# Weight sums on GpSimd alone, hidden tiles paired, and one sum moved back to VectorE: a tuned attention and mixer kernel

## The chip, the cores and the metric

The kernel runs on one core of a Trainium2 chip. The core's engines are TensorE (PE in the profile; its weight loads, PEld, run beside its products), VectorE (DVE), ScalarE (ACT), GpSimd (POOL) and SyncE (SP), which here issues nearly all DMA transfers. Each engine works through its own instructions in the order in which they are written and waits on semaphores for the others.

The metric is the device time of one execution in microseconds (us). Beside the plain runs there is one profiled execution, whose trace gives every instruction's start and duration. Times in the text that look like "at 296.46" are microseconds from the first instruction of that execution. The TensorE clock granted is given as a share of full speed.

## The reference: banded attention, then a mixer

For 4 batches, 8 heads, 768 positions and heads 64 wide, attention sees a band of 31 neighbours and 24 block summaries (maxima of the keys and means of the values over 32 positions):

```python
k_sum = k.reshape(B, H, nb, block, D).max(axis=3)
v_sum = v.reshape(B, H, nb, block, D).mean(axis=3)
scores_l = scale * np.matmul(q, k.transpose(0, 1, 3, 2))
mask_l = np.abs(pos[:, None] - pos[None, :]) < window
scores_s = scale * np.einsum('bhsd,bhnd->bhsn', q, k_sum) + np.log(block)
a = softmax over both
x = np.matmul(a, v_all)
```

The result x (768 positions by 512 channels in each batch) goes through a mixer over positions and one over channels:

```python
h = np.maximum(xt @ w_tok1, 0.0) @ w_tok2        # 768 -> 256 -> 768
u = x + h.transpose(0, 2, 1)
h2 = np.maximum(u @ w_ch1, 0.0) @ w_ch2          # 512 -> 1536 -> 512
return u + h2
```

## The kernel before

**Numbers in two parts.** For accuracy most float32 operands are held as two tiles, a rounded high part and the rest. Three products (high by high, high by low, low by high) stand for one. To "split" a tile means one ScalarE copy and one VectorE or POOL subtraction.

**Batches and slots.** The kernel works in three steady batches b = 0, 1, 2 and a last one. The channel mixer of a batch takes 24 slots: two halves of the positions (512 and 256 of them), each with the 12 tiles f of the 1536 hidden channels. A slot is `ch1` (products hp, into h, line 852) and `ch2` (products acc, line 895). Beside it run the attention steps of batch b + 1, in which `scores` begins with a small clear of a tile e on POOL (MEMSET, line 409), then the first mixer of batch b + 1 (`tok1x`: POOL makes the low parts of xs and ws at line 733 for the products t1q at line 747; `tok2`: products up, line 791). After half 0, `finish` adds the results on VectorE (line 926) and POOL (ot, line 934), and stores them. During batch 0 all weights are loaded as 64-bit words, converted and split; they stay in SBUF, 12 tiles `w1_t[f]` and 12 tiles `w2_t[f]`, tags "w1" and "w2".

**The last batch.** The channel mixer of batch 3 is done with Strassen's scheme in Winograd's form: the matrices are cut into 2 by 2 blocks, and 7 products of blocks do the work of 8. It needs four sums of weight blocks for each of 6 pairs of hidden tiles and both weights: 12 groups s_w_k, w = 1, 2 and k = 0 to 5. `weight_sums` makes a group in ten steps of 128x256 elements (`between`: a tensor_tensor on POOL, line 973, or a scalar_tensor_tensor on VectorE, line 975) and stores it to DRAM ("sums"). `last_mix` reads them back. Its first phase runs k = 0 to 5 (products pa, pb, pc). Each step k uses its two tiles of the first weights for the last time. Their buffers, tag "w1", are a ring of 12, taken in order by the weights of the second phase: `second_loads` reads 21 tiles, r (copies of the second weights) and rs (sums, which `parted` splits on ScalarE and VectorE). The second phase is seven sets of 36 products: qa, qb (sums s2), qc (s3), qb (s1), qa, qb (s4), qc. The right sides of these come from `second`, which splits them on ScalarE and VectorE (x, xs). The last set's right side, t4, is one more subtraction per k, th <- hb, th, done in place after t2 has been split.

**What sets the order.** Work is not issued where the program names it. `Plan` records each piece with its engine, an assumed duration, a rank and its reads and writes, then runs a list schedule and writes the instructions of each engine in the planned order. `rank` decides among pieces that are ready (R_H first, R_BACK last; the sums have R_BACK). `behind` lets a piece be planned only after another, here the slot's ch1 (`state["gate"]`); on the chip it leaves no wait, only a place in the order. A buffer of a ring (tag, number of buffers) is taken over when all users of its previous tile are done, and on the chip this is a wait at the first instruction that touches it, with everything behind it on that engine.

**The sums before.** `SUMS` names the slots: 14 and 17 in batch 0, then 6, 8, 10, 13, 15 and 6, 8, 10, 12, 14. In half 0 a group's result takes two tiles of the ring "t1" (4 buffers, also used by t1 in `tok1x`), in half 1 one tile of the ring "h". Five of the ten steps are POOL's, five VectorE's.

Of the kernel before, what the change touches and what calls it, by code (L numbers as in the profile page):

```python
# [15 lines left out]
ALU = mybir.AluOpType  # L16
# [23 lines left out]
HL = ((0, 0), (0, 1), (1, 0))  # L40

# [148 lines left out]
def tile_attention_mixer(  # L190
# [759 lines left out]
    HALF = NF // 2  # L950
    sd, wd = {}, {}

    def blocks(w, k):

        a, c = ((w1_t, w2_t)[w - 1][f] for f in (k, k + HALF))
# [23 lines left out]
    def weight_sums(w, k, tag):  # L979
# [4 lines left out]
        if tag == "t1":  # L984
            z = [sbuf([P, 2, 256], tag, f"s_{w}_{k}_{n}", 4) for n in range(2)]
            at = [(z[i // 2], i % 2) for i in range(4)]
        else:
            z = sbuf([P, 4, 256], tag, f"s_{w}_{k}", 2)
            at = [(z, i) for i in range(4)]
# [8 lines left out]
        def step(eng, i, left, right, op):  # L998
            add(
                eng, 0.78 if eng == "pool" else 0.38,  # L1000
                lambda: between(eng, own(i)[0](), left[0](), right[0](), op),
                reads=left[1] + right[1], writes=[at[i]], rank=R_BACK, behind=gate,
            )

        step("pool", 0, part("21", 0), part("22", 0), ALU.add)
        step("pool", 0, own(0), part("21", 1), ALU.add)
        step("pool", 0, own(0), part("22", 1), ALU.add)
        step("dve", 2, part("11", 0), part("21", 0), ALU.subtract)
        step("dve", 2, own(2), part("11", 1), ALU.add)
        step("dve", 2, own(2), part("21", 1), ALU.subtract)  # L1010
        step("pool", 1, own(0), part("11", 0), ALU.subtract)
        step("pool", 1, own(1), part("11", 1), ALU.subtract)
        step("dve", 3, part("12", 0), own(1), ALU.subtract)
        step("dve", 3, own(3), part("12", 1), ALU.add)
        for n in range(2):
            view = (lambda n=n: z[n].t) if tag == "t1" else (lambda n=n: z.t[:, 2 * n : 2 * n + 2])
            add(
                "sp", 0.06,
                lambda n=n, view=view: nc.sync.dma_start(
                    out=away.t[:, 2 * n : 2 * n + 2], in_=view()  # L1020
# [78 lines left out]
    def last_mix():  # L1099
# [71 lines left out]
        def first(k, name, bank_, rhs, start):  # L1171
# [4 lines left out]
            else:  # L1176
                slot, c0 = w1_t[k + HALF * (name[0] == "2")], 2 * (name[1] == "2")
# [8 lines left out]
        def second_loads():  # L1186
            for name, _, _ in SECOND:
                for m in range(HALF // 2):
                    slot = wring[name, m] = sbuf([P, 2, 2, 256], "w1", f"r{name}_{m}", NF, F32R)
                    for j in range(2):  # L1190
# [6 lines left out]
                        else:  # L1197
                            away = wd[k + HALF * (name[1] == "2")]
# [86 lines left out]
        def second(name, rhs, to, k):  # L1285
# [5 lines left out]
            if rhs == "t4":  # L1291
                both("pool", src, (hB[k], 0), src, ALU.subtract, R_LATER)
# [380 lines left out]
```

## Time and profile before

| | us |
|---|---|
| median of 3 runs (577.3 to 581.13) | 580.96 |
| profiled execution | 584.92 |
| its span, first to last instruction | 582.4 |
| TensorE busy | 562.4 (97%) |
| VectorE busy | 389.2 (67%) |
| ScalarE busy | 257.4 (44%) |
| POOL busy | 226.0 (39%) |

The mean granted TensorE clock was 0.985. By the trace's rows, the three steady batches reach from about 120 to 485, the first phase of `last_mix` from 485 to 531, its second phase from 527 to 579.

How to read the rows: a row of groups gives line, engine, operation, output <- inputs by the program's names, shapes and count; then busy us in all, mean ns of one, and the idle time of the engine just before them with what ended it. A row of waits gives who waited for whom: us in all, times, the longest. A row of the chain of waits or of the timeline begins with the start and the duration in us; in square brackets stands the engine's idle time before it. A row of windows gives the stretch, its length, and for each engine the busy time and the number of instructions in it, then the clock, the DMA engines' busy share and GB/s. A busy TensorE is not TensorE at its peak, since ends of matmuls are modelled.

### The profile page before, as it was taken

Reading aid. Unit: us, or ns where it says so; the run is one execution under the profiler, and the core shown is the slowest. Engines: PE = TensorE matmul, PEld = TensorE weight load, DVE = VectorE, ACT = ScalarE, POOL = GpSimd, SP = SyncE. Lnnn points to the kernel's source line nnn. Section 1 sums busy time; section 2 is a strip of 40 time slices with the busy share of each in tenths; the row PEclk is TensorE's granted clock in tenths of the full one; section 3 lists DMA queues with packets and bytes.
Section 4 is the critical chain, followed back from the end, with each engine's and each line's share of the span. In section 5 each row is a group of like instructions: output and inputs, shape, how many; then the busy total and the mean of one; then the engine's idle time right before and its main releaser. Section 6 shows DMA issues by size and latency. Waiting matters only on the chain.

```text
span 582.4 us, 12756 instructions
## 1 busy us (share of the span) xinstructions
PE 562.4 (97%) x4629; PEld 491.2 (84%) x4629; DVE 389.2 (67%) x1036; ACT 257.4 (44%) x789; POOL 226.0 (39%) x271
## 2 busy tenths in 40 slices
PE   7899999989989999999999999999999999999897
PEld 4698888768988987878799997777789999999797
DVE  4688889997575346466657526465544884788985
ACT  4668665537373424232242315332233243557452
POOL 0225577753351610203169410032249512446511
PEclk9879999999989999999999999999999999999999
DMA  8953668653747116767685606777687654435321
GB/s 270 319 169 96 198 199 255 214 186 131 224 147 218 35 43 184 181 199 197 210 256 142 129 12 185 151 185 186 184 225 228 178 227 134 148 117 176 130 98 68
DMA packets 133774, 99.52 MB, mean 171 GB/s; under 512 B 88272, under 2 KB 112464, under 8 KB 133712
## 3 DMA queue, kind: packets, MB, share of 16 engines
q1 hardware_dynamic: 133568, 98.52, 57.2%
q8 instruction: 36, 0.59, 0.4%
q14 instruction: 26, 0.21, 0.1%
q10 hardware_dynamic: 144, 0.20, 0.1%
HBM read 68.60 MB, written 28.31 MB: 166 GB/s over the span
## 4 chain that ended last, share of the span: by engine, by line
PE 69%; DVE 12%; DMA 8%; issue 3%; POOL 3%; ACT 2%; SPq 1%; DVEq 0%; ACTq 0%; POOLq 0%
PE acc L895 19%; PE hp L852 18%; PE av L557 4%; PE t1q L747 4%; PE sc L426 3%; DMA w<-in_w_ch 3%; PE pb L1131 3%; PE up L791 3%; PE qa L1131 2%; DMA away<-e 2%; PE pc L1131 2%; PE pa L1131 2%; PE qb L1131 2%; PE qc L1131 2%; DVE wb L1453 2%
## 5 line engine op out<-in xcount | busy, mean ns | idle before, releaser
L895 PE MATMUL acc<-h,w 128*128 128x512 f32 (+1 forms) x864 | 166.0, 341 | 2.5 <-DVE h L869 2.1
L852 PE MATMUL hp<-u,w 128*128 128x512 f32 (+1 forms) x864 | 163.7, 339 | 0.0
L895 PEld LDWEIGHTS acc<-h,w 128*128 128x128 f32 x864 | 133.2, 189 | 23.8 <-DVE h L869 2.8
L852 PEld LDWEIGHTS hp<-u,w 128*128 128x128 f32 x864 | 133.0, 188 | 20.5 <-issue 1.3
L450 ACT ACTIVATE e<-e,den 128x120 f32<-128x120 f32 x192 | 73.3, 384 | 60.2 <-DVE den L440 58.0
L869 DVE SCALAR_TENSOR_TENSOR h<-hp,h 128x512 fp32r<-128x512 f32 (+1 forms) x72 | 39.8, 553 | 67.6 <-ACT h L864 67.4
L864 ACT ACTIVATE h<-hp 128x512 fp32r<-128x512 f32 (+1 forms) x72 | 35.0, 486 | 104.3 <-PE hp L852 98.2
L440 DVE CUSTOM_DVE_ANT_0 e<-sc,mask_sb 128x120 f32<-128x120 f32 x192 | 41.4, 277 | 11.9 <-PE sc L426 10.8
L934 POOL TENSOR_TENSOR ot<-ot,u 128x512 f32<-128x512 f32 (+1 forms) x24 | 23.8, 1018 | 64.2 <-DVE ot L926 57.1
L1482 POOL TENSOR_TENSOR w<-wb,w 128x256 fp32r<-128x256 f32 x48 | 37.6, 802 | 18.1 <-ACT w L1476 17.8
L409 POOL MEMSET e<- 128x48 f32 x16 | 2.2, 138 | 107.6 <-DMA away<-e 42.6
L791 PE MATMUL up<-wt,t 128*128 128x512 f32 (+2 forms) x192 | 39.2, 345 | 0.4 <-DVE u L808 0.3
L973 POOL TENSOR_TENSOR s<-s,w 128x256 f32<-128x256 f32 x48 | 36.8, 768 | 3.4
L450 ACT ACTIVATION_READ_ACCUMULATOR e<-e,den 128x1 f32 x192 | 36.1, 188 | 0.0
L791 PEld LDWEIGHTS up<-wt,t 128*128 128x128 f32 x192 | 30.3, 189 | 3.8 <-DVE u L808 0.8
L733 POOL TENSOR_TENSOR xs<-x,xs 128x512 fp32r<-128x512 f32 x18 | 24.2, 1343 | 19.3 <-ACT xs L728 19.3
L557 PEld LDWEIGHTS av<-v,eT 120*64 120x64 f32 x768 | 25.1, 143 | 7.7 <-issue 4.7
L557 PE MATMUL av<-v,eT 120*64 120x64 f32 x768 | 27.6, 230 | 3.7 <-issue 2.2
L426 PE MATMUL sc<-k,q 64*64 64x120 f32 x768 | 28.9, 277 | 1.8 <-PE et L488 0.7
L426 PEld LDWEIGHTS sc<-k,q 64*64 64x64 f32 x768 | 21.3, 136 | 10.7 <-issue 6.6
L747 PE MATMUL t1q<-xs,ws 128*128 128x256 f32 x216 | 28.8, 284 | 0.1
L1476 ACT ACTIVATE w<-wb 128x256 fp32r<-128x256 f32 x48 | 18.0, 412 | 24.0 <-DVE wb L1453 23.9
(130 smaller groups left out, 900.0 us busy)
## 6 DMA issues: line engine op xcount, KB each, us to landing
w<-in_w_ch SPq DMA_DIRECT2D x48, 256.0 KB
k<-in_kw SPq DMA_DIRECT2D x16, 720.0 KB
v<-in_vw SPq DMA_DIRECT2D x32, 288.0 KB
q<-in_q SPq DMA_DIRECT2D x16, 384.0 KB
sums<-s SPq DMA_DIRECT2D x24, 256.0 KB
away<-e SPq DMA_DIRECT2D x16, 384.0 KB
eT<-away SPq DMA_DIRECT2D x64, 96.0 KB
w2d<-w SPq DMA_DIRECT2D x12, 512.0 KB
```

The costliest lines, as they stand in the source:

```text
L426: nc.tensor.matmul(tiles[j].t[c * QT : (c + 1) * QT, i * NC : (i + 1) * NC], lhsT=qt.t[rows, t * QT : (t + 1) * QT], rhs=kt.t[rows, t, :], ...
L440: nc.vector.tensor_tensor_reduce(out=e.t[:, j, i * P : i * P + NC], in0=tiles[j].t[:, i * NC : (i + 1) * NC], in1=mask_sb[:, mv, :], op0=A ...
L450: nc.scalar.activation(ei, ei, AF.Exp, bias=den_t[n].t[:, 1, T : T + 1], scale=-1.0, accum_out=den_t[n].t[:, 0, T : T + 1],)
L557: nc.tensor.matmul(pv[cs, T], lhsT=eT[:NC, T % (TT // 2), cs], rhs=v.t[:NC, 2 * T + c], start=True, stop=True,)
L747: nc.tensor.matmul(pt.t[:, 2 * P * k : 2 * P * (k + 1)], lhsT=ws[:, wp, T, ks], rhs=xs[:, xp, T], start=(c == 0 and k == 0 and T == 0 and ...
L791: nc.tensor.matmul(pt.t[:, :nt], lhsT=t1.t[:, part, ks], rhs=wt2[w].t[:, k, h0 : h0 + nt], start=(far and k == 0 and i == 0), stop=(k == D ...
L852: nc.tensor.matmul(pt.t[:, :nt], lhsT=w1_t[f].t[:, w, c], rhs=us[c].t[:, part], start=(i == 0), stop=(i == len(ops) - 1),)
L869: lambda: nc.vector.scalar_tensor_tensor(out=h.t[:, 1], in0=pt.t[:, :nt], scalar=0.0, in1=h.t[:, 0].bitcast(F32), op0=ALU.max, op1=ALU.sub ...
L895: nc.tensor.matmul(slot.t[:, c0 : c0 + nt], lhsT=w2_t[f].t[:, w, o * P : (o + 1) * P], rhs=h.t[:, part], start=(f == 0 and w == 0 and part ...
L973: nc.gpsimd.tensor_tensor(out=out_, in0=left, in1=right, op=op)
L1131: nc.tensor.matmul(bank_.t[:, :HS], lhsT=w(i), rhs=x(j), start=first and n == 0, stop=True, skip_group_check=True,)
L1482: lambda hi=hi, lo=lo, source=source: nc.gpsimd.tensor_tensor(out=lo(), in0=source(), in1=hi().bitcast(F32), op=ALU.subtract),
```

## The change

Three things change.

1. All ten steps of a group are POOL's. The groups stand one per slot in slots 6 to 11 (half 0) of batch 1, for the first weights, and of batch 2, for the second. Batch 0 has none. All results take the ring "t1". The assumed duration of a step is 0.82 instead of 0.78 (POOL) and 0.38 (VectorE).
2. The hidden tiles f are loaded in the order of channel blocks 0, 6, 1, 7, 2, 8 and so on, so that the pair of `last_mix`'s step k is tiles 2k and 2k + 1 instead of k and k + 6.
3. t4 is VectorE's instead of POOL's.

```diff
-        a, c = ((w1_t, w2_t)[w - 1][f] for f in (k, k + HALF))
+        a, c = ((w1_t, w2_t)[w - 1][f] for f in (2 * k, 2 * k + 1))
...
-        if tag == "t1":
-            z = [sbuf([P, 2, 256], tag, f"s_{w}_{k}_{n}", 4) for n in range(2)]
-            at = [(z[i // 2], i % 2) for i in range(4)]
-        else:
-            z = sbuf([P, 4, 256], tag, f"s_{w}_{k}", 2)
-            at = [(z, i) for i in range(4)]
+        z = [sbuf([P, 2, 256], "t1", f"s_{w}_{k}_{n}", 4) for n in range(2)]
+        at = [(z[i // 2], i % 2) for i in range(4)]
...
-        step("dve", 2, part("11", 0), part("21", 0), ALU.subtract)
+        step(2, part("11", 0), part("21", 0), ALU.subtract)
...
-                slot, c0 = w1_t[k + HALF * (name[0] == "2")], 2 * (name[1] == "2")
+                slot, c0 = w1_t[2 * k + (name[0] == "2")], 2 * (name[1] == "2")
...
-                            away = wd[k + HALF * (name[1] == "2")]
+                            away = wd[2 * k + (name[1] == "2")]
...
-                both("pool", src, (hB[k], 0), src, ALU.subtract, R_LATER)
+                both("dve", src, (hB[k], 0), src, ALU.subtract, R_LATER)
...
-        fs, ws = slice(f * P, (f + 1) * P), slice(2 * f * P, 2 * (f + 1) * P)
+        at = f // 2 + HALF * (f % 2)
+        fs, ws = slice(at * P, (at + 1) * P), slice(2 * at * P, 2 * (at + 1) * P)
...
-    SUMS = ((14, 17), (6, 8, 10, 13, 15), (6, 8, 10, 12, 14))
...
-            if slot in SUMS[b]:
-                n = len(sd)
-                weight_sums(1 + n // HALF, n % HALF, "t1" if half == 0 else "h")
+            if b and HALF <= slot < NF:
+                weight_sums(b, slot - HALF)
```

The planner then writes other orders. In the names below the first number after s, e or ot is left out: s_4_0 is the first tile of group k = 4, w a weight tile, e a tile of attention weights, and the last number is a running one.

POOL before, batch 1, from the last sums of half 0 to the first mixer's low parts:

```order
L973 TENSOR_TENSOR s_4_0_3581<-w_10_1601 128x256
L973 TENSOR_TENSOR s_4_0_3581<-s_4_0_3581,w_10_1601 128x256
L409 MEMSET e_0_3590 128x6x8
L973 TENSOR_TENSOR s_4_0_3581<-s_4_0_3581,w_10_1601 128x256
L973 TENSOR_TENSOR s_4_0_3581<-s_4_0_3581,w_4_1210 128x256 x2
L409 MEMSET e_1_3723 128x6x8
L934 TENSOR_TENSOR ot_0_0_3788<-ot_0_0_3788,u_0_0_2731 128x512
```

POOL now, the same place:

```order
L410 MEMSET e_1_3713 128x6x8
L973 TENSOR_TENSOR s_4_1_3709<-s_4_1_3709,w_8_1500 128x256
L973 TENSOR_TENSOR s_4_1_3709<-s_4_1_3709,w_9_1556 128x256
L973 TENSOR_TENSOR s_4_0_3667<-s_4_0_3667,w_8_1500 128x256 x2
L973 TENSOR_TENSOR s_4_1_3709<-w_8_1500,s_4_0_3667 128x256
L973 TENSOR_TENSOR s_4_1_3709<-s_4_1_3709,w_8_1500 128x256
L973 TENSOR_TENSOR s_5_0_3792<-w_11_1661 128x256
L935 TENSOR_TENSOR ot_0_0_3786<-ot_0_0_3786,u_0_0_2707 128x512
```

Between the clear of e_1 and ot no sum stood before; now seven steps do. From batch 1's third clear to ot there are 12, 19, 10 and 7 steps behind one clear each, where there were 1, 7, 3 and 0; three steps stand in front of that clear and nine behind ot, xs and ws. In batch 2 the counts are 2 in front of the first clear after slot 6, then 8, 18, 10, 13 and nine behind ot.

VectorE before, in the second phase of `last_mix`, around the right sides of qb (xs <- th) and of qc (xs <- ha):

```order
L975 SCALAR_TENSOR_TENSOR xs_1_6601<-th_6176,xs_1_6601 128x384
L975 SCALAR_TENSOR_TENSOR rs_0_6511<-rs_0_6511 128x2x256
L975 SCALAR_TENSOR_TENSOR xs_2_6614<-th_6335,xs_2_6614 128x384
L975 SCALAR_TENSOR_TENSOR rs_1_6513<-rs_1_6513 128x2x256
L975 SCALAR_TENSOR_TENSOR xs_3_6643<-th_6335,xs_3_6643 128x384
L975 SCALAR_TENSOR_TENSOR xs_4_6649<-th_6491,xs_4_6649 128x384
L975 SCALAR_TENSOR_TENSOR rs_2_6515<-rs_2_6515 128x2x256
L975 SCALAR_TENSOR_TENSOR xs_5_6663<-th_6491,xs_5_6663 128x384
L975 SCALAR_TENSOR_TENSOR rs_0_6517<-rs_0_6517 128x2x256
L975 SCALAR_TENSOR_TENSOR xs_0_6675<-ha_6075,xs_0_6675 128x384
```

VectorE now, the same place:

```order
L975 SCALAR_TENSOR_TENSOR xs_1_6616<-th_6185,xs_1_6616 128x384
L975 SCALAR_TENSOR_TENSOR th_6185<-hb_6157,th_6185 128x384
L975 SCALAR_TENSOR_TENSOR xs_2_6631<-th_6352,xs_2_6631 128x384
L975 SCALAR_TENSOR_TENSOR th_6352<-hb_6239,th_6352 128x384
L975 SCALAR_TENSOR_TENSOR xs_3_6653<-th_6352,xs_3_6653 128x384
L975 SCALAR_TENSOR_TENSOR th_6352<-hb_6321,th_6352 128x384
L975 SCALAR_TENSOR_TENSOR xs_4_6659<-th_6519,xs_4_6659 128x384
L975 SCALAR_TENSOR_TENSOR th_6519<-hb_6408,th_6519 128x384
L975 SCALAR_TENSOR_TENSOR xs_5_6669<-th_6519,xs_5_6669 128x384
L975 SCALAR_TENSOR_TENSOR th_6519<-hb_6492,th_6519 128x384
L975 SCALAR_TENSOR_TENSOR xs_0_6681<-ha_6081,xs_0_6681 128x384
L975 SCALAR_TENSOR_TENSOR rs_2_6590<-rs_2_6590 128x2x256
```

The splits of rs that stood between the xs have moved ahead, into the first phase, but for one here and one in front of the first xs; in their places stand the six t4 (th <- hb, th).

More of the change, by code (lines that the diff above doesn't have):

```diff
@@ L40 @@
 HL = ((0, 0), (0, 1), (1, 0))
+HALF = NF // 2
 HI_MAX = 122879.9921875
@@ L947, in store @@
         )
-    HALF = NF // 2
     sd, wd = {}, {}
     def blocks(w, k):
-        a, c = ((w1_t, w2_t)[w - 1][f] for f in (k, k + HALF))
+        a, c = ((w1_t, w2_t)[w - 1][f] for f in (2 * k, 2 * k + 1))
         lo, hi = slice(0, 256), slice(256, 512)
@@ L977, in between, with weight_sums @@
             )
-    def weight_sums(w, k, tag):
+    def weight_sums(w, k):
         blk, keys = blocks(w, k)
@@ L996, in own, with step @@
             return (lambda: slot.t[:, j]), [at[i]]
-        def step(eng, i, left, right, op):
+        def step(i, left, right, op):
             add(
-                eng, 0.78 if eng == "pool" else 0.38,
-                lambda: between(eng, own(i)[0](), left[0](), right[0](), op),
+                "pool", 0.82,
+                lambda: between("pool", own(i)[0](), left[0](), right[0](), op),
                 reads=left[1] + right[1], writes=[at[i]], rank=R_BACK, behind=gate,
             )
-        step("pool", 0, part("21", 0), part("22", 0), ALU.add)
-        step("pool", 0, own(0), part("21", 1), ALU.add)
-        step("pool", 0, own(0), part("22", 1), ALU.add)
-        step("dve", 2, part("11", 0), part("21", 0), ALU.subtract)
[L1009 to L1014, printed above, removed]
+        step(0, part("21", 0), part("22", 0), ALU.add)
+        step(0, own(0), part("21", 1), ALU.add)
+        step(0, own(0), part("22", 1), ALU.add)
+        step(2, part("11", 0), part("21", 0), ALU.subtract)
+        step(2, own(2), part("11", 1), ALU.add)
+        step(2, own(2), part("21", 1), ALU.subtract)
+        step(1, own(0), part("11", 0), ALU.subtract)
+        step(1, own(1), part("11", 1), ALU.subtract)
+        step(3, part("12", 0), own(1), ALU.subtract)
+        step(3, own(3), part("12", 1), ALU.add)
         for n in range(2):
-            view = (lambda n=n: z[n].t) if tag == "t1" else (lambda n=n: z.t[:, 2 * n : 2 * n + 2])
             add(
                 "sp", 0.06,
-                lambda n=n, view=view: nc.sync.dma_start(
-                    out=away.t[:, 2 * n : 2 * n + 2], in_=view()
+                lambda n=n: nc.sync.dma_start(
+                    out=away.t[:, 2 * n : 2 * n + 2], in_=z[n].t
                 ),
```

## The prediction

> **What bounds the kernel now.** I read the page first, then busy time by windows, TensorE's own waits, the chain of waits, the groups by line and form, and VectorE's and POOL's timelines.
>
> ```profile
> span 582.4 us, 12756 instructions
> PE 562.4 (97%) x4629; PEld 491.2 (84%) x4629; DVE 389.2 (67%) x1036; ACT 257.4 (44%) x789; POOL 226.0 (39%) x271
> ```
>
> The windows, one row for each stretch:
>
> ```profile
> core 0: us, PE busy (x) PEld busy (x) DVE busy (x) ACT busy (x) POOL busy (x), PEclk, DMA share, GB/s
> ...
> 210.00:295.00 85.00, 85.00 (x678) 67.83 (x678) 50.20 (x180) 26.85 (x108) 14.51 (x25) 1.00 0.65 180
> ...
> 430.00:470.00 40.00, 39.48 (x333) 38.20 (x331) 26.26 (x46) 15.44 (x34) 30.50 (x28) 1.00 0.76 231
> ...
> 485.30:531.00 45.70, 45.70 (x263) 45.70 (x262) 34.43 (x60) 24.25 (x56) 19.29 (x19) 1.00 0.47 148
> 531.00:550.00 19.00, 15.82 (x84) 13.85 (x82) 18.45 (x21) 11.63 (x24) 14.13 (x11) 1.00 0.46 146
> ```
>
> TensorE is the bound: 562.4 of 582.4 us. The change leaves its products in number and shape as they are, so only its idle 20 us are at stake, and most of them lie where the change does nothing (the start, the weight loads). In the batches it hardly idles: not at all in 210:295, 0.5 us in 430:470. The window 531:550 differs: TensorE idles 3.2 us and VectorE is busy 18.45 of 19. There VectorE is the bound. TensorE's waits and the chain of waits say the same:
>
> ```profile
> PE qb L1131 <- DVE xs L975: 2.0, 3, 0.8
> ...
> PE qc L1131 <- DVE xs L975: 1.2, 2, 0.6
> ...
> PE et L488 <- DVE x L570: 1.0, 2, 0.7
> ```
>
> ```profile
> 170.39 1.49 DVE s L975
> ...
> 173.56 0.86 DVE s L975
> ...
> 531.61 4.25 PE qa L1131 x24
> ...
> 553.21 6.24 PE qb L1131 x36
> ```
>
> In last_mix the products qa end at 531.61 + 4.25 = 535.86, and the second set of 36 qb starts at 553.21. Between them stand 72 products, two sets of 36. The set that begins at 553.21 takes 6.24 (the 24 qa, at 4.25, make it 6.4), so 12.5 of those 17.35 us are work and **4.9 are waiting**, for VectorE's split xs. The other wait that bears on this change is in batch 0: transposes of e wait 1.0 us in all for VectorE's x, and on the chain in front of that x stand steps of the weight sums (1.49 and 0.86).
>
> **The change part by part.** First the prices.
>
> ```profile
> L973 POOL TENSOR_TENSOR s<-s,w 128x256 f32<-128x256 f32 x48 | 36.8, 768 | 3.4
> L975 DVE SCALAR_TENSOR_TENSOR s<-s,w 128x256 f32<-128x256 f32 x36 | 21.2, 590 | 0.8
> L975 DVE SCALAR_TENSOR_TENSOR s<-w,s 128x256 f32<-128x256 f32 x12 | 7.1, 595 | 0.8 <-POOL s L973 0.8
> ...
> L973 POOL TENSOR_TENSOR th<-hb,th 128x384 f32<-128x384 f32 x12 | 15.4, 1293 | 2.0 <-DVE xs L975 1.5
> L975 DVE SCALAR_TENSOR_TENSOR xs<-th,xs 128x384 fp32r<-128x384 f32 x12 | 10.4, 884 | 0.3 <-ACT xs L1044 0.3
> L975 DVE SCALAR_TENSOR_TENSOR x<-ha,x 128x384 fp32r<-128x384 f32 x6 | 3.1, 552 | 0.2 <-ACT x L1044 0.2
> L975 DVE SCALAR_TENSOR_TENSOR rs<-rs 128x512 fp32r<-128x512 f32 x12 | 11.0, 919 | 0.6 <-ACT rs L1143 0.5
> 550.33 0.68 DVE L975 SCALAR_TENSOR_TENSOR rs<-rs 128x512 fp32r<-128x512 f32 x1
> 171.80 0.71 DVE L563 SCALAR_TENSOR_TENSOR rec<-den 128x6 f32<-128x6 f32 x1
> 298.94 0.15 DVE L563 SCALAR_TENSOR_TENSOR rec<-den 128x6 f32<-128x6 f32 x1
> ```
>
> *Sums off VectorE.* Twelve groups of ten steps; half of the 120 steps leave VectorE (60 at about 0.59, some 35 us) and come to POOL at 0.768. Nearly all of what VectorE loses lay beside TensorE's work, since TensorE hardly waits there. What it pays: in batch 0 the sums vanish from slots 14 and 17, and with them the 1.0 us of TensorE's wait for x. I take −1.0 (between 0, if another step is then late, and −2.4, the two sums on the chain). Around the end of batch 2, where VectorE also loses sums, TensorE idles 0.5 us; that is the most that goes there, and I leave it to pay for what comes next.
>
> *Sums on POOL.* Each of batches 1 and 2 now has 60 steps there, from slot 6 on. Whether they fit is read from POOL's own row of waits and steps, since POOL works in written order: the clears of e (MEMSET) must wait for their slot, and sums stand between them.
>
> ```profile
> 253.61 0.14 POOL L409 MEMSET e<- 128x48 f32 x1 [12.30 <-DVE s L975]
> ...
> 263.14 0.14 POOL L409 MEMSET e<- 128x48 f32 x1 [8.71 <-PE av L557]
> 264.04 3.25 POOL L973 TENSOR_TENSOR s<-s,w 128x256 f32<-128x256 f32 x4
> 280.27 0.14 POOL L409 MEMSET e<- 128x48 f32 x1 [11.47 <-DMA away<-e]
> 289.22 0.14 POOL L409 MEMSET e<- 128x48 f32 x1 [6.50 <-PE av L557]
> 296.46 2.55 POOL L934 TENSOR_TENSOR ot<-ot,u 128x512 f32<-128x512 f32 x2 [7.10 <-ACT e L450]
> 388.15 0.14 POOL L409 MEMSET e<- 128x48 f32 x1 [3.98 <-DMA away<-e]
> 410.13 0.14 POOL L409 MEMSET e<- 128x48 f32 x1 [11.05 <-DMA away<-e]
> 430.80 2.54 POOL L934 TENSOR_TENSOR ot<-ot,u 128x512 f32<-128x512 f32 x2 [12.74 <-DVE ot L926]
> 456.19 3.72 POOL L973 TENSOR_TENSOR s<-s,w 128x256 f32<-128x256 f32 x4
> ```
>
> A step costs 3.25 / 4 = 0.81 from start to start. In batch 1 the new order puts 12, 19, 10 and 7 steps behind the four clears that now start at 253.61, 263.14, 280.27 and 289.22. From 253.7, 12 steps end at 263.5 (0.4 behind the next clear's time), 19 at 279.0 (clear at 280.27), 10 at 288.5 (289.22), 7 at 295.0, in front of ot at 296.46. The nine left over stand behind the first three pairs xs, ws, where ten stood before. In batch 2 it is 8 and 18 steps from 388.15 to 410.13 (26 × 0.81 = 21.1, of 22.0), then 10 and 13 up to ot at 430.80 (23 × 0.81 = 18.6, of 20.7). So POOL is full and in time, by one or two us in forty: I take 0 for the halves' first parts. If it is late, xs and ws behind ot are late, and TensorE's t1q with them. If steps keep the 3.72 / 4 = 0.93 that the last four took, beside VectorE's sums, ot comes 2.2 late in batch 1 and 3.3 in batch 2: 5.5 us at most. At the end of batch 2 six steps instead of three stand in front of the second half's pairs xs, ws, 3 × 0.81 = 2.4 us; TensorE has had hp and acc moved ahead there, so I take 0.5, the idle time saved above, and let the two cancel (0 to 2.4).
>
> The Trainium skill speaks against this move: in "GPSIMD Engine Reference", Engine selection, it gives elementwise work on a tile to VectorE and calls GpSimd about twice as slow with two inputs. The rows agree in direction (0.768 against 0.59). By that rule POOL, not TensorE, would set the pace of these slots; what that gives here is the second rival.
>
> *VectorE beside a full POOL.* A reciprocal's first step, rec, took 0.71 beside POOL's sums and 0.15 without. With 8 of these in each batch, 8 × 0.56 = 4.5 us come onto VectorE, which has 35 idle in 210:295. I take 0.
>
> *t4 on VectorE.* Six of the twelve th on POOL, 1.29 each, go to VectorE. No row has t4 there; its nearest is x<-ha, same size and operation, 0.552 (upper bound: 0.884, as xs runs now beside POOL). So VectorE gets 6 × 0.55 = 3.3 more in the stretch where it is the bound, but the splits xs next to it fall from 0.884 to 0.552.
>
> *Channel tiles in pairs.* The order of f in ch1 and ch2 costs nothing: same tiles, same loads, others' columns. Its effect is in last_mix: step k frees two neighbouring slots of the ring "w1" instead of slots k and k + 6, so loads r and rs, which take that ring in order, come twice as early, and their splits on VectorE with them. Of six rs splits that stood among the twelve xs behind qa, two remain.
>
> *The sum for 535.86 to 553.21.* For the first set VectorE has 6 xs and 6 t4, 12 × 0.552 = 6.6, against TensorE's 6.24; for the second 6 xs, one rs (0.68) and two sums out_a (0.55 each by x<-ha): 5.1 against 6.24. Before it was 12 × 0.884 + 6 × 0.919 + 1.1 = 17.2, which is the 17.35 seen. So TensorE is the bound again but for 0.4 us at the start, and 4.9 − 0.4 = 4.5 go; with POOL's last th still beside the first xs, I take **−4.3** (0 to −4.9). The five other rs splits fall into 485:531, where VectorE is busy 34.4 of 45.7: 5 × 0.919 = 4.6 more, 85%. A bank's evacuation can then stand behind a split: I take +0.5 (0 to 2).
>
> The sum: −1.0 − 4.3 + 0.5 − 0.5 + 0.5 = **−4.8 us**. The profiled execution took 584.92 us, its span 582.4; it becomes about 580.1. The median of the runs shown is 580.96, 4 us lower, and 580.96 − 4.8 = 576.2, 0.8% less. A measurement of this kernel tells about 1% (5.8 us) from no change.
>
> **The rivals.**
>
> *VectorE stays the bound in last_mix.* For it: 11.7 us of work against 12.5 is close, the first phase gets fuller, and xs could keep 0.884 while POOL ends its last th. Against: six POOL instructions that ran beside xs are gone. With xs and t4 at 0.884 the first set takes 12 × 0.884 = 10.6, 4.4 more than TensorE's 6.24; 0.5 of the 4.9 is gained, and with batch 0 the time is about 579.5. Chance 0.2.
>
> *POOL runs late by contention* (0.93 for a step): TensorE has 0.7 to 1.5 us to spare at t1q, so of 5.5 about 4 reach it: 576.2 + 4 = 580. Chance 0.15.
>
> *Stores hold up the sums: slower.* Tiles of the sums stand in the ring "t1" of four, two for each group, so group k + 2 waits until the stores of group k have landed, and SP issues those in written order, behind loads of k and q.
>
> ```profile
> 381.64 6.46 DMA away<-e
> ...
> 466.61 3.90 DMA w2d<-w
> ```
>
> Sizes, by the page's list of DMA issues:
>
> ```profile
> k<-in_kw SPq DMA_DIRECT2D x16, 720.0 KB
> q<-in_q SPq DMA_DIRECT2D x16, 384.0 KB
> sums<-s SPq DMA_DIRECT2D x24, 256.0 KB
> away<-e SPq DMA_DIRECT2D x16, 384.0 KB
> ```
>
> The store away<-e landed 6.46 us after its issue, w2d<-w after 3.90. From a tile's last step to its next first step there are 12 steps, 9.7 us. While issue and landing stay below that, nothing waits; with 3.5 us more on SP in front of them, every reuse (four in each batch) costs up to 3 us, 12 in a batch. About 1.5 are spare before ot and 0.7 at t1q, so TensorE loses some 10 in each batch: 576.2 + 20 = 596, or 586 if half of the reuses are late. It decides at 9.7 us from a tile's last step to its landing. For it speaks that in each batch some stores stand right behind a k and a q: 720 + 384 + 256 KB at the 180 GB/s of 210:295 are 7.6 us. Against: the others don't, and 6.46 and 3.90 stay below 9.7. Chance 0.15.
>
> **How the numbers follow.** Forecast 0.5, VectorE still the bound 0.2, POOL late 0.15, stores 0.15. The likeliest gives 576.2; its own range goes from 573 (2.4, 4.9 and 0.5 gained, nothing paid) to 580 (most of the bounds paid). The other cases are 579.5, 580 and 586 to 596. With the 4 us by which the runs shown differ, 571 to 585 holds all but the stores' case and a tail. More than 1% faster means below 575.2: somewhat under half of the forecast, 0.22, and 0.06 by the spread of runs from the neighbours, 0.28. Slower by over 1% (above 586.8) is the stores' case but for its mild end, and accidents of order: 0.14. Within 1%: 0.58.
>
> **What would show it.** In the changed profile: TensorE's waits for xs (2.0 and 1.2) gone or below 1 in all, and the next 36 qb starting about 13 us after qa's end instead of 17.35; xs at 0.55 to 0.65; rs splits before qa. No wait of et for x in batch 0. POOL busy without a gap from slot 6 to ot in batches 1 and 2, with ot at most 1 us later than VectorE's part of it, and t1q not waiting for ws. If POOL's sums wait for DMA sums<-s in most groups, the stores' case is right. I am wrong altogether if TensorE waits at t1q or at av in batch 1 or 2, or if VectorE's evacuations hold banks in 485:531.

## The result, and the profile after

The changed kernel takes 571.42 us (median of 4 runs, 569.56 to 572.01). The kernel before took 579.91 in its four runs (577.3 to 581.13). The ratio is 0.9854, 95% interval 0.9809 to 0.9899: 8.5 us less, between 5.9 and 11.1. By the prediction's bound of 1% that is faster. The prediction was 4.8 us less, 576.2. Its wide range, 571 to 585, just holds the time; the likeliest case's own range, 573 to 580, doesn't, and "within 1%", which had the highest chance (0.58), didn't come. Two executions of e6 below, 675.51 us at a TensorE clock of 0.75 and 1308.95 us, are slow ones, and no figure here rests on them.

The profiled execution of the changed kernel took 569.56 us, 1.9 below its median; that of the kernel before took 584.92, 5.0 above its own. The spans therefore differ by 14.8 us, which is more than the change is worth. Some of this lies in the first 60 us, where the instructions are the same: TensorE's clock there was 0.87 and 0.90 before (windows 0:30 and 30:60) and 1.0 after. Some lies in the second half of batch 0, which is taken up under e4.

The page's first lines after:

```profile
span 567.6 us, 12757 instructions
PE 552.1 (97%) x4629; PEld 485.3 (85%) x4629; DVE 355.6 (63%) x982; ACT 258.2 (45%) x789; POOL 258.9 (46%) x325
```

VectorE has lost 33.6 us and POOL has gained 32.9. To see where TensorE gained, I cut each span at the starts of the same products: the first hp of each half, the first pa, and the second set of qb behind qa in `last_mix`. A row of this table is the time from one such start to the next, read from the timelines; the last column is the rest of the span. (The first hp of batch 0 starts at 68.48, so the steady batches begin there and not at about 120.)

```
                    to     batch 0        batch 1        batch 2        pa to   rest
                 1st hp  half 0 half 1  half 0 half 1  half 0 half 1  2nd qb
before            68.48   69.07  74.67   80.97  53.28   81.12  57.57   67.88  29.39
changed           65.53   68.56  71.01   80.97  52.50   81.05  55.24   63.22  29.55
```

Between batch 1 and the end there are four differences: -0.78 in the second half of batch 1, -0.07 and -2.33 in batch 2, and -4.66 in `last_mix`. The first half of batch 1 is the same to the hundredth of a microsecond, although POOL now does all its sums there. The windows of the second half of batch 2, before and then after (the columns are those of the prediction's windows):

```profile
427.60:485.17 57.57, 56.52 (x470) 54.73 (x468) 35.41 (x67) 20.34 (x46) 30.50 (x28) 1.00 0.63 197
```

```profile
419.62:474.86 55.24, 55.24 (x470) 54.50 (x468) 28.57 (x57) 20.60 (x46) 29.71 (x28) 1.00 0.66 207
```

TensorE does the same 470 products, in a somewhat different order (the planner's two orders part in the second half of batch 1). Of the 2.33 us only 57.57 - 56.52 = 1.05 stood as idle time before; the other 1.28 was in its busy time. The time from the start of one product to the start of the next shows where: before, ten such steps are longer than usual (0.12 for hp and acc, 0.17 for up) by 2.3 us together, and each is at a product that waits for u or h, or right beside one. All other steps take the same time in both profiles to within 0.03 us in all, so the order itself costs nothing. Three rows of TensorE's timeline before show the waits, and three of VectorE's show who was late:

```profile
459.85 5.76 PE L791 MATMUL up<-wt,t 128*128 128x384 f32 x30 [0.27 <-DVE u L808]
470.17 0.50 PE L895 MATMUL acc<-h,w 128*128 128x256 f32 x2 [0.40 <-ACT h L864]
471.03 1.46 PE L895 MATMUL acc<-h,w 128*128 128x256 f32 x10 [0.35 <-DVE h L869]
...
453.87 2.66 DVE L975 SCALAR_TENSOR_TENSOR u<-u,u 128x384 fp32r<-128x384 f32 x1 [1.48 <-ACT u L818]
...
457.33 0.97 DVE L975 SCALAR_TENSOR_TENSOR s<-w,s 128x256 f32<-128x256 f32 x1
...
470.56 0.41 DVE L869 SCALAR_TENSOR_TENSOR h<-hp,h 128x256 fp32r<-128x256 f32 x1
```

From 456 to 474 VectorE's timeline shows no idle time. Seven steps of sums stand there, from 456.92 to 463.8, among the evacuations of up (u), t and hp (h), and single instructions beside POOL's took up to 2.66 us. After, the sums are not there, and VectorE waits for ScalarE in front of an h instead:

```profile
457.30 0.42 DVE L870 SCALAR_TENSOR_TENSOR h<-hp,h 128x256 fp32r<-128x256 f32 x1 [0.22 <-ACT h L865]
```

In batch 1 four long steps make 0.7 of the 0.78 us: two at `up`, which waits for VectorE's x behind steps of the sums, and two at `t1q`, which waits for POOL's ws behind four steps of sums. No view of waits lists them, since each gap is under 0.15 us.

In `last_mix`, the chain of waits after:

```profile
521.30 4.24 PE qa L1126 x24
525.54 6.36 PE qb L1126 x36
531.90 6.34 PE qc L1126 x36
538.24 6.29 PE qb L1126 x36
```

From qa's end (525.54) to the second qb (538.24) it is 12.70 us where it was 17.35. TensorE's waits for xs, 2.0 and 1.2 before, are gone from its list. VectorE's timeline at that place:

```profile
523.03 1.31 DVE L975 SCALAR_TENSOR_TENSOR xs<-th,xs 128x384 fp32r<-128x384 f32 x1
524.38 1.26 DVE L975 SCALAR_TENSOR_TENSOR th<-hb,th 128x384 f32<-128x384 f32 x1
525.56 0.55 DVE L975 SCALAR_TENSOR_TENSOR xs<-th,xs 128x384 fp32r<-128x384 f32 x1
526.14 0.56 DVE L975 SCALAR_TENSOR_TENSOR th<-hb,th 128x384 f32<-128x384 f32 x1
```

The first two run beside POOL's last two instructions there, th and ha, and take 1.3; the later ones of these twelve take 0.55.

### The profile page after: what moved, and what is told of

The parts are those of the page before. It is cut to its first block, busy times and chain, and to the rows that moved or that the text cites. A ratio compares the mean times of both kernels' runs of the same rounds, so it can differ in the third digit from the quotient of the medians.

```text
span 567.6 us, 12757 instructions
## 1 busy us (share of the span) xinstructions
PE 552.1 (97%) x4629; PEld 485.3 (85%) x4629; DVE 355.6 (63%) x982; ACT 258.2 (45%) x789; POOL 258.9 (46%) x325
## 4 chain that ended last, share of the span: by engine, by line
PE 76%; DVE 11%; DMA 6%; ACT 3%; issue 2%; POOL 1%; SPq 1%; ACTq 0%; DVEq 0%
PE acc L896 21%; PE hp L853 20%; PE t1q L748 5%; PE up L792 4%; PE av L558 4%; PE pb L1126 3%; PE qb L1126 3%; PE sc L427 3%; DMA w<-in_w_ch 3%; PE qa L1126 2%; PE pc L1126 2%; PE pa L1126 2%; PE qc L1126 2%; DVE wb L1449 2%; ACT e L451 1%
## 5 line engine op out<-in xcount | busy, mean ns | idle before, releaser
L973 POOL TENSOR_TENSOR s<-s,w 128x256 f32<-128x256 f32 x84 | 61.7, 741 | 5.0
```

What stands on the lines that cost most here:

```text
L973: nc.gpsimd.tensor_tensor(out=out_, in0=left, in1=right, op=op)
```

## The experiments

The theory after the result: the gain is in four places (batch 0, the two second halves, `last_mix`), and in the second halves it comes from no sums standing there, not from POOL doing them. The rivals: that POOL alone matters; that batch 0 holds most of it; that POOL or the stores are near a limit. Each ratio is to the kernel before on the same chip. The table of stages, for all of them whose profile is used:

```
                    to     batch 0        batch 1        batch 2        pa to   rest
                 1st hp  half 0 half 1  half 0 half 1  half 0 half 1  2nd qb
e1_t4             65.05   68.66  70.31   80.97  53.96   80.58  57.56   63.93  29.75
e2_pairs          68.25   70.50  72.70   80.97  53.28   80.83  57.56   64.72  29.72
e3_sums           65.64   68.80  72.01   80.97  52.50   80.98  55.24   67.90  29.74
e4_b0             65.24   68.75  71.59   80.97  53.28   80.33  57.58   67.93  29.63
e5_t4pool         67.59   69.11  70.11   80.97  52.50   80.77  55.24   64.75  29.51
e7_allpool        65.97   70.85  70.07   80.97  52.50   81.68  57.15   67.94  29.51
e8_twice          65.34   69.49  71.39   80.97  54.70   81.61  58.80   63.25  29.62
e9_stores         67.02   69.23  71.76   78.36  59.82   81.86  61.31   75.28  29.52
e10_stores2       67.42   68.61  69.92   80.97  52.50   82.12  61.83   63.25  29.64
e11_half0         64.94   69.51  72.41   80.00  53.56   80.75  55.22   63.25  29.63
e12_mixed         65.27   70.56  71.61   80.00  53.90   80.66  56.22   63.21  29.40
```

(In the runs e11 and e12, 24 of TensorE's products sc stand in the second half of batch 1 instead of the first, so the two halves are to be read together.)

### One part at a time

**e1_t4**: the kernel before with t4 on VectorE.

```diff
-                both("pool", src, (hB[k], 0), src, ALU.subtract, R_LATER)
+                both("dve", src, (hB[k], 0), src, ALU.subtract, R_LATER)
```

> The kernel before with one change: t4 on VectorE. From the end of the 24 qa to the start of the second set of qb it took 17.35 us before and 12.70 after. If the splits xs are slow because POOL works beside them, VectorE has 14 xs and t4 at 0.55, six rs at 0.68 to 0.92 and 1.1 for two sums: 12.9 to 14.3, so 3.0 to 4.4 us go and the ratio to before is 0.993 to 0.995. If 0.884 is what an xs costs by itself, t4 only adds to VectorE: 19 us there, 1.7 us slower, ratio 1.003. Nothing else changes.

577.73 us, ratio 0.9949 (0.9922 to 0.9977). From pa to the second qb it is 63.93 instead of 67.88, so 3.95 went, as the first theory says: an xs is slow because of POOL, and moving work onto the engine that is the bound made that engine faster. Up to `last_mix` the instructions of TensorE, VectorE, ScalarE and POOL are those of before in the same order, which makes its table row useful twice: it shows how far the same instructions differ from one execution to the next. Its second half of batch 0 took 70.31, where before it was 74.67; its second half of batch 1 took 53.96, where it was 53.28. The 0.68 is one wait at `up`. A step of the sums on VectorE stood 1.45 us for POOL's step, x stood behind it, and `up` behind x:

```profile
306.48 0.95 DVE L975 SCALAR_TENSOR_TENSOR s<-w,s 128x256 f32<-128x256 f32 x1 [1.45 <-POOL s L973]
...
308.23 0.55 DVE L570 TENSOR_TENSOR x<-av,rec 128x384 f32<-128x384 f32 x1
...
308.92 2.97 PE L791 MATMUL up<-wt,t 128*128 128x512 f32 x12 [0.84 <-DVE x L570]
```

**e2_pairs**: the kernel before with only the hidden tiles paired.

```diff
-        a, c = ((w1_t, w2_t)[w - 1][f] for f in (k, k + HALF))
+        a, c = ((w1_t, w2_t)[w - 1][f] for f in (2 * k, 2 * k + 1))
...
-        fs, ws = slice(f * P, (f + 1) * P), slice(2 * f * P, 2 * (f + 1) * P)
+        at = f // 2 + HALF * (f % 2)
+        fs, ws = slice(at * P, (at + 1) * P), slice(2 * at * P, 2 * (at + 1) * P)
```

> The kernel before with one change: hidden tiles paired as 2k and 2k + 1, in both the loads and last_mix. The prediction's term: four of the six rs splits leave the stretch between the qa and the second set of qb, VectorE keeps 12 xs at 0.884, one or two rs and 1.1, that is 12.6 against TensorE's 12.5; the 17.35 us become about 13 and 4.3 go, ratio 0.9925. Rival: the t4 on POOL hold the splits up (xs and th of one tile follow each other), then the stretch stays above 15 us and less than 2.4 go. The batches stay as before: 150 to 180 us as before, the end of batch 2 as before.

577.24 us, ratio 0.9960 (0.9933 to 0.9987). The stretch is 64.72: 3.16 went, not 4.3. Against the changed kernel (63.22) 1.5 us are missing, nearly all of it in the second of the two sets. The cause is seen on VectorE and then on TensorE, and the groups by line name the instruction beside it:

```profile
532.26 7.77 DVE L975 SCALAR_TENSOR_TENSOR xs<-th,xs 128x384 fp32r<-128x384 f32 x6
...
543.26 5.70 PE L1131 MATMUL qc<-xs,rs 128*128 128x384 f32 x29 [0.57 <-DVE xs L975]
...
L973 POOL TENSOR_TENSOR th<-hb,th 128x384 f32<-128x384 f32 x12 | 15.2, 1283 | 0.5
```

Six xs take 7.77, 1.29 each, as long as the th on POOL (1.283). TensorE needs only 6.24 for them: 7.77 - 6.24 = 1.5.

**e5_t4pool**: the changed kernel with t4 back on POOL, the edit of e1 reversed.

> The changed kernel with t4 on POOL again. The paired tiles alone left 64.7 us from the first pa to the second qb, against 63.2 in the changed kernel and 67.9 before: here too 64.7, batches as in the changed kernel, so 1.5 us over it, ratio to before 0.988. By the prediction's own sum for VectorE (12 xs at 0.884 and one rs, 12.6 against 12.5) the t4 on POOL cost nothing: 63.2, ratio 0.985.

572.04 us, ratio 0.9852 (0.9805 to 0.9899). The stretch is 64.75, as in e2, so t4 on VectorE is worth 1.5 us of the profile once the tiles are paired. The ratios can't show so little (0.9854 and 0.9852). Either edit alone takes most of the wait in `last_mix`; they overlap.

**e3_sums**: the changed kernel with the tiles paired as before and t4 on POOL, so that only the sums on POOL in slots 6 to 11 are left.

> The changed kernel with tiles paired as before (k and k + 6) and t4 on POOL again: of the change only the sums on POOL in slots 6 to 11 are left. The prediction's terms: -1.0 in batch 0 (0 to -2.4) and nothing in batches 1 and 2, last_mix as before with 17.35 us between qa and the second qb; ratio 0.998. Rival, from the profile after: TensorE gains about 4 us in batch 0 between 150 and 180 and about 2 at the end of batch 2, so -6 in all, ratio 0.990.

574.67 us, ratio 0.9898 (0.9875 to 0.9921). `last_mix` is as before (67.90), and the sums' part is worth 5.9 us (4.6 to 7.2), not the 1.0 of the prediction: the rival's -6. The table gives 0.78 of it in batch 1 and 2.33 + 0.14 in batch 2; the rest lies ahead of batch 1, or in the spread of the runs.

### Batch 0

**e4_b0**: the kernel before with the two groups of batch 0 moved to slot 5 of the other batches.

```diff
-    SUMS = ((14, 17), (6, 8, 10, 13, 15), (6, 8, 10, 12, 14))
+    SUMS = ((), (5, 6, 8, 10, 13, 15), (5, 6, 8, 10, 12, 14))
```

> The kernel before with the two groups of sums taken out of batch 0 alone and put in slot 5 of batches 1 and 2; five steps of ten stay on VectorE. If batch 0's gain comes from the sums not being there, it is here as well: -1.0 by the prediction, -4 by the rival that the sums there delay more than x (the loads of k and v for the next heads, and av with them); ratio 0.998 or 0.993. If the gain needs VectorE free of sums later on too, nothing goes here, ratio 1.0.

578.52 us, ratio 0.9971 (0.9949 to 0.9994): 1.7 us less, between 0.3 and 3.0. Batches 1 and 2 keep their waits (53.28 and 57.58). So -1.0 and -4 lie on either side of it, and -4 is outside its interval. The wait that the prediction's -1.0 rested on didn't go with the sums: et waits for x 1.4 us in this run and 1.2 in e3, with no sums in batch 0, 0.5 in the changed kernel, and 0.3 to 2.3 in the four profiles that have them (before, e1, e2, e11).

One profile can't size this stage. Most of the 4.36 us between before and e1 is seen in three places: a gap of 2.20 us in front of av at 162.28, for which the profile shows no wait (0.7 in e1); TensorE's clock at 0.50 for the next 3.4 us, which costs 1.7; and the wait for x (1.0 against 0.3).

```profile
162.10:165.50 3.40, 3.22 (x58) 3.14 (x62) 1.85 (x8) 1.94 (x11) 0.00 (x0) 0.50 0.30 80
```

In the four profiles with two groups half on VectorE there (before, e1, e2, e11) its second half takes 70.31 to 74.67, mean 72.5; in the eight without any (changed, e3, e4, e5, e8, e9, e10, e12) 69.92 to 72.01, mean 71.2. The means differ by 1.3, or by 0.9 when the 1.7 us of clock in before is taken out. With the two groups still there, but all on POOL (e7), it takes 70.07.

### POOL, or the place

**e7_allpool**: the kernel before, its slots kept, all steps on POOL.

```diff
+            eng = "pool"
             add(
-                eng, 0.78 if eng == "pool" else 0.38,
+                eng, 0.82,
```

> The kernel before, its slots kept (two in batch 0, and in batches 1 and 2 some in the second half), but all ten steps of a group on POOL. If VectorE's steps are what holds up TensorE in the second halves, they fall to 52.5 and 55.2 us here too, and the two groups in batch 0 cost VectorE nothing: ratio 0.992 to 0.995. If it is the place, POOL's steps now stand among its low parts xs and ws of the second halves: 20 steps in batch 1 and 20 in batch 2 at 0.75 are 15 us in stretches where POOL was busy 29.6 of 50 and 30.5 of 40, so t1q waits for ws in batch 2 for up to 5 us: ratio 0.997 to 1.003.

578.23 us, ratio 0.9957 (0.9929 to 0.9985). Both theories get half. In batch 1 the second half falls to 52.50. In batch 2 it stays at 57.15, though VectorE has no steps of those sums any more, and t1q doesn't wait for ws either. The wait is this one, and VectorE's rows ahead of it:

```profile
468.05 1.45 PE L895 MATMUL acc<-h,w 128*128 128x256 f32 x10 [1.64 <-DVE h L869]
...
463.40 2.12 DVE L975 SCALAR_TENSOR_TENSOR u<-u,u 128x384 fp32r<-128x384 f32 x2
465.44 1.09 DVE L975 SCALAR_TENSOR_TENSOR t<-t,t 128x384 fp32r<-128x384 f32 x1
```

POOL works on sums until 466 here, and beside them the u and t of VectorE, 0.54 to 0.56 in e11 at the same work, take 1.06 and 1.09. VectorE comes late to h.

**e6_mixed**, and once more as **e12_mixed**: the changed kernel with five of ten steps on VectorE, in the new slots.

```diff
         def step(i, left, right, op):
+            eng = "dve" if i > 1 else "pool"
             add(
-                "pool", 0.82,
+                eng, 0.82 if eng == "pool" else 0.38,
```

> The changed kernel, but five of a group's ten steps (tiles 2 and 3 of a group) are VectorE's again; the slots 6 to 11 stay. In the profiles so far the second half of batch 1 takes 53.28 us before and 52.50 after, that of batch 2 57.57 and 55.24. If that gain of 3.1 comes from no sums standing among VectorE's evacuations in the second halves, it stays whichever engine makes the sums in the first halves: 52.5 and 55.2, first halves 81 as always, and the ratio to before is that of the changed kernel, 0.985. If POOL must have all of them, VectorE's steps beside POOL's make e or h late in the first halves, 1 to 3 us in each, and the ratio is 0.988 to 0.995.

> The same kernel as the one with five of ten steps on VectorE in slots 6 to 11, once more, since its profile fell on a disturbed execution. Place theory: first halves 81, second halves 52.5 and 55.2, last_mix's first part 63.2, ratio 0.985. Against the run with two groups left in batch 0 it differs by these two groups: by the prediction's term -1.0, by the run that took them out alone -1.7.

e6 took 573.4 us (the middle of four runs, 570.10 to 576.33), ratio 0.9870 (0.9809 to 0.9931), and e12 571.41, ratio 0.9849 (0.9800 to 0.9898). The profile is that of e12. Batch 1 takes 133.90 and batch 2 136.88, where before they took 134.25 and 138.69 and in the changed kernel 133.47 and 136.29. VectorE is busy 53.1 of 80.65 us in the first half of batch 2 and TensorE doesn't notice. So 2.2 of the 3.2 us are kept. The place theory's 55.2 for the second half of batch 2 was missed by 1.0: it takes 56.22, and TensorE waits for h at 469, much as it did before the change. VectorE makes no sums there; ScalarE had stood 4.50 us up to 463 for a tile of sums that was being read back, the kind of wait that e10 shows.

**e11_half0**: paired tiles and t4 on VectorE, the sums half and half and two groups in batch 0 as before; only the slots of the others are new.

```diff
-    SUMS = ((14, 17), (6, 8, 10, 13, 15), (6, 8, 10, 12, 14))
+    SUMS = ((14, 17), (6, 7, 8, 9, 10), (6, 7, 8, 9, 10))
```

> Paired tiles and t4 on VectorE as in the changed kernel, but the sums by POOL and VectorE half and half as before, two groups in batch 0 as before, the others in slots 6 to 10 of batches 1 and 2: of the move of the sums only the place is left. If the place decides, the second halves take 52.5 and 55.2 us, last_mix's first part 63.2, and with batch 0 as before the ratio is 0.986 to 0.989. If VectorE must be free of sums altogether, 53.3 and 57.6 stay, or the first halves grow above 81: 0.992.

571.40 us, ratio 0.9865 (0.9811 to 0.9919): that of the changed kernel (0.9854) within the intervals, without a single step more on POOL. Batch 1 takes 133.56, batch 2 135.97. Its window of the second half of batch 2:

```profile
421.18:476.40 55.22, 55.22 (x470) 54.49 (x469) 29.02 (x62) 20.92 (x49) 22.43 (x18) 1.00 0.62 191
```

So the place decides in batches 1 and 2: the gain is there with half of the steps on VectorE (e11), and only in part with all of them on POOL in the old slots (e7). It isn't the order of products either: in e11 thirty `up` stand in one row as they did before, and take 5.37 us without a wait where they took 5.76. Which engine makes the sums in the first halves doesn't matter within what these runs can tell. What the two groups of batch 0 cost can't be read from e11 and e12: the ratios differ by 0.0016, and each is known to about 0.005.

### How near the limits are

**e8_twice**: two of a group's ten steps done twice, the planner not told.

```diff
+            def run():
+                for _ in range(2 if len(left[1]) > 1 and (i == 0 or i == 2) else 1):
+                    between("pool", own(i)[0](), left[0](), right[0](), op)
             add(
-                "pool", 0.82,
-                lambda: between("pool", own(i)[0](), left[0](), right[0](), op),
+                "pool", 0.82, run,
```

> The changed kernel, with two of a group's ten steps done twice (the first step of tiles 0 and 2, the same result again), in an order of instructions otherwise the same. POOL gets 12 x 0.81 = 9.7 us more in slots 6 to 11 of each batch. By the prediction POOL is full with one or two us to spare (after: idle 0.83 before ot in batch 1, 2.73 in batch 2): ot is 8.9 and 7.0 late, 0.7 to 1.5 are spare at t1q, so the second halves grow by about 7.5 and 5.5: 13 us over the changed kernel, ratio to before 1.008. If POOL has more room than that (clears of e wait for their slots 5 to 10 us in all, half of which the steps can fill), some 3 to 6 us come, ratio 0.990 to 0.996.

577.89 us, ratio 0.9941 (0.9910 to 0.9973), some 5 us over the changed kernel. The second halves take 2.20 and 3.56 more, 5.8 together, where the prediction's "full and in time by one or two us" makes 13. POOL's timeline shows where the room was, in the changed kernel and then here:

```profile
272.19 0.74 POOL L973 TENSOR_TENSOR s<-w 128x256 f32<-128x256 f32 x1 [4.39 <-DMA sums<-s]
...
289.34 2.55 POOL L935 TENSOR_TENSOR ot<-ot,u 128x512 f32<-128x512 f32 x2 [0.83 <-ACT e L451]
```

```profile
273.11 1.55 POOL L973 TENSOR_TENSOR s<-w 128x256 f32<-128x256 f32 x2 [0.32 <-DMA sums<-s]
...
293.46 2.53 POOL L935 TENSOR_TENSOR ot<-ot,u 128x512 f32<-128x512 f32 x2
```

A wait for a store of 4.39 us is filled to 0.32, and ot comes 6.26 after the first hp of the half (287.20) instead of 3.27 (286.07): 3.0 late for 9.7 us more work.

**e9_stores**: each tile of the sums stored a second time, as a piece of its own.

```diff
+            add(
+                "sp", 0.06,
+                lambda n=n: nc.sync.dma_start(
+                    out=spare.t[:, 2 * n : 2 * n + 2], in_=z[n].t
+                ),
+                reads=at[2 * n : 2 * n + 2], writes=[(spare, n)], kb=262,
+            )
```

> The changed kernel, with each tile of the sums stored twice, the second time to a place that nobody reads: 256 KB more for each group. Tests the prediction's third rival at the point where it decides. One step of the changed kernel already waited 4.39 us for sums<-s. With the second stores a tile is free later by their own time, 1.5 to 3 us each at 180 GB/s: if the ring is at its limit, most of the four reuses in each batch wait 2 to 4 us, POOL comes to ot 5 to 10 late, and TensorE loses 8 to 16: ratio 0.999 to 1.013. If there is slack (only the stores behind k and q are late), one or two more waits show on POOL, and TensorE loses 0 to 2: ratio 0.985 to 0.989.

594.74 us, ratio 1.0240 (1.0188 to 1.0291), worse than either theory. (A store is 256 KB and a group has two, so the second stores are 512 KB a group, twice what was expected here and in e10.) It isn't a clean test: the planner counted the new pieces and wrote another order (part of batch 1's products moved to its second half). On POOL still only one step waits for a store, 3.78 us. **e10_stores2** therefore issues both stores in the old piece, and TensorE, VectorE and POOL keep the changed kernel's order.

```diff
-                lambda n=n: nc.sync.dma_start(
-                    out=away.t[:, 2 * n : 2 * n + 2], in_=z[n].t
-                ),
+                lambda n=n: [
+                    nc.sync.dma_start(out=to.t[:, 2 * n : 2 * n + 2], in_=z[n].t)
+                    for to in (away, spare)
+                ],
```

> The changed kernel, each tile of the sums stored twice, the second time to a place that nobody reads; unlike in the run with separate store pieces, the order of instructions on TensorE, VectorE and POOL is that of the changed kernel, only SP issues 24 stores more. If the ring t1 is at its limit (the third rival), the second stores (256 KB a group, 1.5 us at 180 GB/s, more behind k and q) make POOL's first steps of a group wait in most of the four reuses of a batch, POOL comes to ot 3 to 8 us late, and the second halves of batches 1 and 2 grow by 2 to 7 us each: ratio to before 0.995 to 1.010. If the one wait seen (4.39 us, behind k and q) is the only place where a store is late, that wait grows by 2 to 4 us, POOL's room of about 4 us takes most of it, and TensorE loses 0 to 2: ratio 0.985 to 0.989. What was lost in that other run (11.7 us before the second qb, 13 in the second halves) was then the other order and the other traffic.

577.61 us, ratio 0.9939 (0.9904 to 0.9974): 5 us over the changed kernel, a little under the least that the third rival was given (0.995), and not by its mechanism. POOL waits once, 4.59 instead of 4.39, and batch 1 is unchanged (80.97, 52.50). The loss is 1.07 in the first half of batch 2 and 6.59 in the second, and it begins on SP, where the load that reads the sums back (line 1159) is issued only after a second store has landed; the two stores are one piece here, so this wait is the edit's own. From the chain of waits, ScalarE's timeline and TensorE's:

```profile
457.93 4.58 DMA spare<-s
462.58 0.32 SPq L1159
...
465.15 0.42 ACT L1140 ACTIVATE s<-s 128x256 fp32r<-128x256 f32 x1 [4.81 <-DMA s<-sums]
...
471.04 0.55 PE L896 MATMUL acc<-h,w 128*128 128x256 f32 x2 [1.82 <-ACT h L865]
472.43 2.50 PE L896 MATMUL acc<-h,w 128*128 128x256 f32 x10 [0.84 <-DVE h L870]
```

ScalarE stands 4.81 us at the split of s, with u and h behind it, and TensorE waits for h. In e11, by contrast, POOL's first steps of a group waited 13.6 us for stores, in two waits, without any cost to TensorE:

```profile
L973 POOL TENSOR_TENSOR s<-w,w 128x256 f32<-128x256 f32 x6 | 4.7, 783 | 14.2 <-DMA sums<-s 13.6 <-DVE den L440 0.7
```

## Why the prediction came out as it did

**Batch 0, -1.0 (0 to -2.4).** The size is not contradicted, and not settled to better than its bounds: -1.7 in e4 (0.3 to 3.0), -0.9 by the means of the profiles with the clock taken out. The mechanism is not borne out. The prediction let TensorE's wait for x vanish with the sums; 0.5 of its 1.0 us is left in the changed kernel, and e3 and e4, with no sums there, wait 1.2 and 1.4. It took that wait from one profile, of a stage that differs by 4.4 us between two executions of the same instructions. That the size fits is luck as far as these runs show; what the sums cost there stays open.

**Sums off VectorE in batches 1 and 2, at most -0.5. This is the step that failed.** The term measured -0.78 in batch 1 and -2.40 in batch 2, 3.2 us in all. The prediction named the steps of VectorE's sums at the end of batch 2 as something to lose, and then bounded their price by TensorE's idle time in 430:470, 0.5 us. Two things were wrong with that bound. The half ends at 485, not 470, and another 0.5 us of idle time lay in that piece. And the busy time was itself longer by 1.28 us for the same 470 products, so idle time is no upper bound for what waiting costs: the products around a late one show longer busy rows (the ten long steps above). In batch 1 the same holds: the window 295:345 showed 0.2 us idle, and 0.78 went. The prediction then let the 0.5 cancel against six sums in front of the second half's pairs xs, ws; no cost of those shows in the two second halves.

**Sums on POOL, 0.** Right for what the change asks: the first halves take 80.97 and 81.05 where they took 80.97 and 81.12, and ot starts 0.83 and 2.73 us after POOL has become free. The walk along the clears had the counts right (12, 19, 10 and 7 steps); a step came after 0.78 instead of 0.81 (twelve from 246.39 to 255.73), and the margin was larger than the "one or two us": 9.7 us more in each batch cost 5.8 in the two together (e8). POOL was not busy without a gap, as it waited once for 4.39 us. The Trainium skill's rule, in "GPSIMD Engine Reference", Engine selection, that elementwise work on a tile belongs to VectorE, doesn't decide the kernel's time here in either direction: with half of the steps on VectorE the ratios are 0.9865 (e11) and 0.9849 (e12), with all of them on POOL 0.9854. About the instruction itself the rule has the direction right, as two groups of e11 show, POOL's steps and VectorE's, though beside each other they differ by 1.4 times and not by two:

```profile
L973 POOL TENSOR_TENSOR s<-s,w 128x256 f32<-128x256 f32 x48 | 37.0, 772 | 3.5
L975 DVE SCALAR_TENSOR_TENSOR s<-s,w 128x256 f32<-128x256 f32 x36 | 20.3, 565 | 0.9
```

**VectorE beside a full POOL, 0.** Right: TensorE lost nothing in the first halves.

**t4, the pairs and last_mix, -4.3 (0 to -4.9).** Right: -4.66. The parts were right too, xs at 0.55 and rs ahead of qa, and the reason for t4 is confirmed by e1 (63.93). What the sum didn't say is that its two parts overlap: t4 alone takes 3.95 and the pairs alone 3.16. The 0.4 us taken off for a wait at the start didn't come; the first xs starts at 523.03, 2.5 us ahead of the first qb.

**The first phase, +0.5 (0 to 2).** It cost nothing. From the first pa to the first qb it is 50.52 us before and after. VectorE is 3.2 us busier there (the prediction's sum had 4.6), 83% of the stretch; the windows before and then after:

```profile
485.17:535.69 50.52, 50.52 (x291) 50.52 (x290) 38.70 (x64) 28.18 (x64) 23.19 (x23) 1.00 0.47 149
...
474.86:525.38 50.52, 50.52 (x291) 50.52 (x290) 41.87 (x69) 30.32 (x68) 23.32 (x22) 1.00 0.48 150
```

**The rivals.** VectorE isn't the bound in `last_mix`. POOL isn't late. The stores do hold up a step of the sums once, behind loads of k and q as the prediction said, but the 4.39 us are absorbed, and doubling the stores moves that wait by 0.2. The price of the doubled stores was at another place, where the sums are read back (e10).

**The sum.** By the table batches 1 and 2 and `last_mix` give -0.8, -2.4 and -4.7, and with -0.9 for batch 0 the sum is -8.8, against a measured -8.5 (5.9 to 11.1). Of what lies beyond the predicted -4.8, batches 1 and 2 (3.2) are the most; the two costs of 0.5 and 0.4 that didn't come are about the rest.

## What to carry to other kernels

Idle time of the bounding engine in a window was no bound on what its waits cost here: compare the length of the same piece of work (from one product to the same product later) with and without them, and cut the window at the borders of the work. Background work belongs where the engines that serve the bound have room, and its place counted for more here than its engine. When a stage's length differs between two profiles of the same program, take its price from timed runs and not from one trace.

## What the runs showed of the hardware

In `last_mix` VectorE's xs, with two inputs in SBUF, went at the pace of the POOL instruction beside it: in e2 six xs took 1.29 us each beside th (1.283), and in the changed kernel 0.55 without. The Trainium skill says in "SBUF — State Buffer", Who interferes with whom, that a VectorE instruction with two SBUF inputs contends with a GpSimd instruction that reads SBUF. The trace agrees, and it shows what follows for a planner: moving a subtraction (t4) from POOL to VectorE gave VectorE more to do, and the stretch that it bounds became 3.95 us shorter (e1).

A wait can cost more than its length. In e10, with TensorE's two waits of 1.82 and 0.84 close together, its granted clock then stood at half for 6.8 us:

```profile
471.40:478.20 6.80, 5.96 (x29) 5.77 (x28) 4.66 (x12) 2.23 (x5) 0.00 (x0) 0.50 0.14 57
```

This loses up to 6.8 x 0.5 = 3.4 us, beside waits of 2.66, and the half grew by 6.59. The length of a wait alone doesn't tell whether the clock falls. The shorter waits of the kernel before (0.35 to 0.81 in the second halves and in `last_mix`) left it at 1.0, and so did one of 1.64 in e7. Near 120 us, in batch 0, a product acc waits 1.79 or 1.80 us for h in eight of the thirteen profiles. In three of them (e2, e7, e12) the clock then stood at 0.5 for 3.4 us, in the other five (before, e5, e8, e9, e11) it stayed at 1.0; those three have the longest first halves of batch 0 in the tables, 70.50 to 70.85 where the others take 68.56 to 69.51. The start of the program, where TensorE waits for its first loads, shows the same from execution to execution: 68.48 us up to the first hp at a clock of 0.87 to 0.90, 65.53 at 1.0.
